# The 1024x1024 weight w3 transposed by DMA instead of TensorE, with the loads ordered behind the transposes

## The chip, the core and the metric

The kernel runs on one core of a Trainium2 chip. A core has TensorE (PE, with PEld for its weight loads), VectorE (DVE), ScalarE (ACT), GpSimd (POOL) and SyncE (SP), and 16 DMA engines that all queues share. Here GpSimd issues the loads from HBM (which cast float32 to bfloat16 on the way), SyncE issues the DMA transposes and almost all stores. The metric is the device time of one execution in microseconds. Before the change it is 581.21 us, the median of 8 runs (580.31 to 581.56).

## The reference

```python
def _attn_ref(q, k, v, tau):            # q, k, v: (4, 5824, 256) float32, tau = 1
    qn = q / (np.linalg.norm(q, axis=1, keepdims=True) + 1e-06)
    kn = k / (np.linalg.norm(k, axis=1, keepdims=True) + 1e-06)
    s = kn.transpose(0, 2, 1) @ qn / tau        # (4, 256, 256)
    s = s - s.max(-1, keepdims=True)
    a = np.exp(s)
    a /= a.sum(-1, keepdims=True) + 1e-09
    return (v @ a)

def _moe_ref(x, w1, w2, w3, w_out):     # x: (23296, 256); w1, w2: (256, 1024)
    a = x @ w1
    b = x @ w2
    h = a * b @ w3                      # (a * b) @ w3, w3: (1024, 1024)
    return (h @ w_out)                  # w_out: (1024, 256)
```

For each of four batches a 256x256 channel attention matrix is formed from q and k (sums over all 5824 rows), applied to v, and a feed-forward layer with a product of two branches follows.

## The kernel before, in words

**Folding.** The kernel never forms x = v @ a. It folds the attention matrix into the two first weights, once per batch: Wf = (softmax matrix) @ [w1, w2], 256 x 2 x 1024 (`fold_mm`, line 337). It also folds the last two weights, once in all: W_sb = w3 @ w_out, 1024 x 256 (`w_unit`, line 567). For that product w3 has to lie transposed in SBUF. So each batch is: a = v Wf1, b = v Wf2, ab = a * b, out = ab W_sb.

**Chunks and steps.** A batch's 5824 rows are 45 tiles of 128 rows and a rest of 64; they are taken in 12 chunks (`NCH`), eleven of 512 columns and a short one of 192. For each chunk there are eight steps j (`emit_ab`, line 413): four TensorE products of 512 columns into two PSUM tiles a and b; ScalarE copies a to SBUF (line 425); VectorE multiplies with b into a bfloat16 tile `ab` (line 428). The out product of a step (`emit_out`, line 438) is four products of 256 columns, issued later: finished `ab` tiles wait in the list `pend`, of which two steps stay (`LAG`). After the eighth step of a chunk ScalarE and VectorE copy the sums out of PSUM and SyncE stores them (512 KB). As long as W_sb is not ready (`w_ready`), `pend` only grows; later up to two out steps per a/b step are issued until it is down to two. 38 `ab` buffers hold this backlog.

**Inputs.** q, k and v come in six pieces per batch (piece = 8 row tiles, 512 KB in bfloat16, the last one shorter): 5 buffers for q, 6 for k, 3 for v. v is needed transposed (vT): a piece is loaded, and SyncE issues a DMA transpose of it (`transpose_piece`, line 149). Pieces 0 and 1 of batch 0 are transposed on TensorE (`transpose_half_on_pe`). vT piece p serves chunks 2p and 2p+1. The buffers of vT are two; the first one holds w3 and w_out in the beginning (`w3_wout`, line 490).

**Order of the work.** The order on each engine is the order of the program; each engine runs its own instructions in order and waits by semaphores. Batch 0's scores are formed at the start, ahead of everything (lines 485 to 556). Then a planner runs: `clock` adds up TensorE's cost in microseconds (a/b step 0.863, out step 0.437), and an agenda (`make_agenda`, line 582) holds side work with a due time on that clock: loads, DMA transposes, the score products of the next batch (`score_units`: 69 units, spread from t0 to t1), its soft-max (`soft_units`), and in batch 0 the transposes of w3 (`w3_transpose`, due from 12 us) and the eight `w_unit` products (due from 24 us). `run_due` issues what is due before each step.

**Gates.** A load would start as soon as GpSimd reaches it. `gate` (line 408) holds it back: GpSimd copies one element of the newest `ab` tile, so GpSimd waits until VectorE has made that tile, and the load that follows in GpSimd's order starts then.

**w3 before.** w3 is loaded in two transfers (line 536), then w_out, then piece 2 of v. `w3_transpose` (line 559) turns each 128-row block by eight TensorE transposes into a PSUM tile of the "ab" buffers, which ScalarE or VectorE (in turn) copies to SBUF: 64 transposes, eight copies. Two halves of the result lie in `sq` buffers, two in a `Wf` buffer.

Of the kernel before, what the change touches and what calls it, by code (L numbers as in the profile page):

```python
# [13 lines left out]
BF16 = DT.bfloat16  # L14

P = 128
# [8 lines left out]
def kernel(  # L25
# [102 lines left out]
    def pe_transpose(dst, src, tag, on_act):  # L128

        m = psum.tile([P, 8, P], BF16, tag=tag, name=f"tr_{nc.get_next_instruction_name()}", bufs={"ab": 4, "out": 3}[tag])  # L130
        for i, blk in enumerate(src):
            nc.tensor.transpose(m[:, i, :], blk, ident_b)
# [256 lines left out]
    def at(t, cost, fn):  # L389
        seq[0] += 1  # L390
        agenda.append((t, seq[0], cost, fn))
# [12 lines left out]
        return vTt[:, ct, :]  # L404

    last_ab = [None]

    def gate():

        if last_ab[0] is not None:  # L410
            nc.gpsimd.tensor_copy(gate_t, last_ab[0][:1, :1])  # L411

    def emit_ab(b, c, j):
        n = chunk_cols(c)
        tiles = []
        for w in range(2):
            t = psum.tile([P, 512], F32, tag="ab", name=f"{'ab'[w]}_{b}_{c}_{j}", bufs=4)
            for ct in range(CT):
                nc.tensor.matmul(  # L419
                    t[:, :n], lhsT=Wf[b][:, ct, w, j * P : (j + 1) * P], rhs=rhs_of(b, c, ct),  # L420
                    start=(ct == 0), stop=(ct == CT - 1),
                )
            tiles.append(t)
        a_sb = work.tile([P, 512], BF16, tag="a_sb", name=f"as_{b}_{c}_{j}", bufs=4)
        nc.scalar.copy(a_sb[:, :n], tiles[0][:, :n])  # L425
        ab = work.tile([P, 512], BF16, tag="ab_sb", name=f"abs_{b}_{c}_{j}", bufs=8 * NDEF + 6)
        if n == 4 * P:
            nc.vector.tensor_mul(ab, a_sb, tiles[1])  # L428
# [50 lines left out]
    def load_qk(n, pi):  # L479
        load_piece("q", n, pi)  # L480
        load_piece("k", n, pi)
# [11 lines left out]
    w3T = {}  # L493

    def new_w3T():

        m = wf_pool.tile([P, 2, 2, FT, P], BF16, tag="Wf", name="w3T_wf")
        for h in range(2):
            w3T[h] = work.tile([P, 2, FT, P], BF16, tag="sq", name=f"w3T_{h}", bufs=2)
            w3T[2 + h] = m[:, h]  # L500

    w3r = moe_w3.rearrange("(jh jl) l -> jl jh l", jl=P)
    w1r = moe_w1.rearrange("(ch cl) f -> cl ch f", cl=P)
# [27 lines left out]
            new_piece("v", 0, 0)  # L531
        load_part("v", 0, 0, h * half, (h + 1) * half)
    load_piece("v", 0, 1)
    for h in range(2):
        js = slice(h * FT // 2, (h + 1) * FT // 2)
        nc.gpsimd.dma_start(out=w3_bf[:, js, :], in_=w3r[:, js, :])
    nc.gpsimd.dma_start(out=wout_sb, in_=moe_w_out.rearrange("(lh ll) c -> ll lh c", ll=P))
    load_piece("v", 0, 2)
    squares("k", 4, whole)
    squares("k", 5, range(LAST + 1), end=True)  # L540
    soft0[0]()
# [12 lines left out]
    busy(4)  # L554
    transpose_half_on_pe(0, 0, 0, False)
    soft0[4]()
    new_w3T()

    def w3_transpose(jt):
        pe_transpose(  # L560
            w3T[jt // 2][:, jt % 2, :, :], [w3_bf[:, jt, lt * P : (lt + 1) * P] for lt in range(FT)],
            "ab", jt % 2 == 0,
        )

    w_ready = [False]

    def w_unit(jt):
# [14 lines left out]
    def make_agenda(b):  # L582
        agenda.clear()
        clock[0] = 0.0
        n = b + 1
        if b == 0:
            for i in range(2):
                at(1.5 + 0.6 * i, 0.43, soft0[5 + i])
            at(4.0, 0.5, lambda: transpose_half_on_pe(0, 0, 1, False))
            at(7.0, 0.5, lambda: transpose_half_on_pe(0, 1, 0, True))  # L590
            at(8.0, 0.5, lambda: transpose_half_on_pe(0, 1, 1, False))
            for jt in range(FT):
                at((12.0 if jt < 4 else 15.0) + jt, 0.5, lambda jt=jt: w3_transpose(jt))
                at(24.0 + jt, 0.87, lambda jt=jt: w_unit(jt))
            at(14.0, 0.0, lambda: transpose_piece(0, 2))
            loads = [("v", 0, 3, 14.0), ("v", 0, 4, 34.0), ("v", 0, 5, 54.0)]
            loads += [("qk", 1, pi, t) for pi, t in enumerate([22.0, 30.0, 40.0, 52.0, 66.0, 80.0])]
            loads += [("v", 1, pi, t) for pi, t in enumerate([96.0, 108.0, 122.0])]
            t0, t1 = 52.0, 120.0
        else:  # L600
            loads = [("v", b, pi, t) for pi, t in [(3, 1.0), (4, 20.0), (5, 34.0)]]
            t0, t1 = 16.0, 104.0
            if n < B:
                loads += [("qk", n, pi, t) for pi, t in enumerate([4.0, 12.0, 27.0, 44.0, 58.0, 72.0])]
                loads += [("v", n, pi, t) for pi, t in enumerate([84.0, 96.0, 108.0])]
        for nm, m, pi, t in loads:
# [68 lines left out]
```

## Time and profile before

| | |
|---|---|
| median of 8 runs | 581.21 us (580.31 to 581.56) |
| the profiled execution, its own time | 581.51 us |
| its span in the profile | 579.1 us |
| TensorE busy | 565.1 us (98%) |
| VectorE, ScalarE, GpSimd busy | 376.8, 341.5, 64.1 us |
| software DMA queue (loads) / hardware queue (stores, transposes) | 39.46 MB / 34.61 MB |
| a, b products, 128x512 | 704 each, 379 ns each by the profile |
| out products, 128x256 | 1440, 273 ns each |
| first a/b step of batch 0, 1, 2 | 40.38, 187.19, 321.39 us |

A matmul's duration in the profile includes its way through the array, and matmuls overlap; what one costs TensorE is read from the distance of starts (two products of 512 columns: 0.43 us). In a timeline line, the first number is the start in us from the span's begin, the second the time, and in brackets stands the idle time before, and what ended it. In a stretch, each engine has its busy time and its number of instructions; then come the granted clock, the DMA engines' share and GB/s. In lists of DMA issues the last number is the median time in us from issue to landing.

### The profile page before, as it was taken

The page shows a single profiled execution, that of the slowest core. Times are in us where ns is not written, and L with a number is a line of the kernel's source. Part 1 is how long each engine was busy: PE and PEld are TensorE (multiplying, and loading weights), DVE is VectorE, ACT ScalarE, POOL GpSimd, SP SyncE. Part 2 cuts the span into 40 slices and gives each one's busy share as a digit, 9 for nine tenths or more (in the row PEclk, how much of TensorE's full clock was granted, in tenths as well). Part 3 has the DMA queues.
Part 4 walks back from the last instruction along what each step waited for, and adds up shares of the span by engine and source line. Part 5 has one row for each costly group of instructions (what it writes and reads, how often), then busy time and mean ns, then how long its engine had stood idle before and what let it go on. Part 6 is the DMA issues. An engine that isn't in the chain of part 4 may idle for free.

```text
span 579.1 us, 10224 instructions
## 1 busy us (share of the span) xinstructions
PE 565.1 (98%) x3826; PEld 360.7 (62%) x3834; DVE 376.8 (65%) x601; ACT 341.5 (59%) x628; POOL 64.1 (11%) x142
## 2 busy tenths in 40 slices
PE   7799999999999999999999999999999999999996
PEld 4665676766656566666666666666665655566664
DVE  0047545888877667788766667778876656565564
ACT  0046535777765566777665566767665555454453
POOL 5240021110000202001000112001100000000000
PEclk9999999999999999999999999999999999999999
DMA  8999989773543899755552699754563335301011
GB/s 163 212 207 199 172 155 204 163 166 77 122 98 109 127 224 176 116 110 125 123 132 74 141 200 173 172 113 87 146 130 89 83 78 144 84 38 74 37 72 55
DMA packets 66113, 74.85 MB, mean 129 GB/s; under 512 B 45840, under 2 KB 49808, under 8 KB 66064
## 3 DMA queue, kind: packets, MB, share of 16 engines
q0 software_dynamic: 15376, 39.46, 40.0%
q1 hardware_dynamic: 50544, 34.61, 20.6%
q8 instruction: 30, 0.49, 0.3%
q14 instruction: 19, 0.16, 0.1%
q10 hardware_dynamic: 144, 0.13, 0.1%
HBM read 78.91 MB, written 23.86 MB: 177 GB/s over the span
## 4 chain that ended last, share of the span: by engine, by line
PE 87%; DMA 7%; ACT 1%; DVE 1%; issue 1%; POOL 1%; ACTq 0%; POOLq 0%
PE o L452 26%; PE a L419 26%; PE b L419 26%; PE G L188 5%; DMA q<-in_q_dram 4%; DMA k<-in_k_dram 2%; PE fold L344 2%; PE w L570 1%; DMA v<-in_v_dram 1%; ACT as L425 1%; DVE abs L428 1%; POOL k L109 0%; DVE osb L473 0%; PE row L272 0%; POOL q L109 0%
## 5 line engine op out<-in xcount | busy, mean ns | idle before, releaser
L428 DVE TENSOR_TENSOR abs<-as,b 128x512 bf16<-128x512 bf16 x352 | 240.4, 685 | 148.6 <-ACT as L425 137.8
L425 ACT CAST as<-a 128x512 bf16<-128x512 f32 (+1 forms) x384 | 215.5, 562 | 173.2 <-PE a L419 84.0
L452 PE MATMUL o<-W_sb,abs 128*128 128x256 bf16 x1440 | 218.1, 273 | 0.5 <-ACT osb L472 0.4
L419 PEld LDWEIGHTS <-Wf 128*128 128x128 bf16 x1536 | 148.9, 98 | 98.1 <-issue 1.7
L419 PE MATMUL a<-vT,Wf 128*128 128x512 bf16 x704 | 209.4, 379 | 0.4
L419 PE MATMUL b<-vT,Wf 128*128 128x512 bf16 x704 | 209.4, 379 | 0.1
L452 PEld LDWEIGHTS <-abs 128*128 128x128 bf16 x1440 | 140.7, 98 | 86.2 <-issue 0.5
L197 DVE TENSOR_TENSOR acc<-acc,sq 128x1024 f32<-128x1024 f32 x66 | 80.4, 1218 | 0.1
L411 POOL COPY gate_t<-abs 1x1 bf16<-1x1 bf16 x39 | 10.3, 265 | 395.6 <-DVE abs L428 387.5
L188 PE MATMUL G<-k,q 128*128 128x256 bf16 x276 | 49.7, 273 | 0.5 <-DMA k<-in_k_dram 0.5
L185 ACT ACTIVATE sq<-q 128x512 f32<-128x512 bf16 x66 | 41.8, 633 | 0.0
L185 ACT ACTIVATE sq<-k 128x512 f32<-128x512 bf16 x66 | 41.6, 631 | 0.0
L473 DVE COPY osb<-o 128x512 f32<-128x512 f32 x44 | 30.1, 684 | 0.4 <-PE o L452 0.4
L188 PEld LDWEIGHTS <-q 128*128 128x128 bf16 x276 | 27.0, 98 | 3.8 <-issue 0.7
L472 ACT COPY osb<-o 128x512 f32<-128x512 f32 x44 | 25.7, 585 | 3.8 <-PE o L452 1.7
L274 ACT ACTIVATE kr<-row 128x256 f32<-128x256 f32 x4 | 1.5, 384 | 31.1 <-PE row L272 31.1
L109 POOL DMA_DIRECT2D q<-in_q_dram x28 | 15.0, 538 | 13.8 <-DMA k<-in_k_dram 5.0
L344 PE MATMUL fold<-w,e 128*128 128x512 bf16 x61 | 16.0, 378 | 0.1
L351 ACT ACTIVATE Wf<-fold,rs 128x512 bf16<-128x512 f32 x16 | 10.9, 687 | 8.4 <-PE fold L344 5.5
L109 POOL DMA_DIRECT2D v<-in_v_dram x25 | 13.4, 539 | 6.7 <-issue 4.9
L109 POOL DMA_DIRECT2D k<-in_k_dram x25 | 13.8, 551 | 3.4 <-DMA k<-in_k_dram 1.9
L353 DVE TENSOR_SCALAR Wf<-fold,rs 128x512 bf16<-128x512 f32 x16 | 11.8, 747 | 2.2 <-PE fold L344 1.8
(103 smaller groups left out, 196.4 us busy)
## 6 DMA issues: line engine op xcount, KB each, us to landing
out_dram<-osb SPq DMA_DIRECT2D x44, 512.0 KB, 3.0
k<-in_k_dram POOLq DMA_DIRECT2D x19, 512.0 KB, 9.2
v<-in_v_dram POOLq DMA_DIRECT2D x19, 512.0 KB, 5.3
q<-in_q_dram POOLq DMA_DIRECT2D x18, 512.0 KB, 6.6
w_wout<-in_moe_w_dram POOLq DMA_DIRECT2D x2, 1024.0 KB, 16.2
k<-in_k_dram POOLq DMA_DIRECT2D x4, 320.0 KB, 6.5
v<-in_v_dram POOLq DMA_DIRECT2D x4, 320.0 KB, 5.2
q<-in_q_dram POOLq DMA_DIRECT2D x4, 256.0 KB, 10.4
```

The source lines that it names most:

```text
L109: nc.gpsimd.dma_start(out=pieces[nm, n, pi][:, lo:hi, :], in_=qk_main[nm, n][0][:, pi * PIECE + lo : pi * PIECE + hi, :])
L185: nc.scalar.activation(out=dst[:, :, part, :], in_=src[:, o : o + 2, :], func=AF.Square)
L188: nc.tensor.matmul(G[:, ct, :], lhsT=qt[:, i, ct * P : (ct + 1) * P], rhs=kt[:, i, :], start=(pr == 0 and part == 0 and ct == 0), stop=(pr ...
L197: nc.vector.tensor_add(accs[n], accs[n], sqs[0])
L344: nc.tensor.matmul(st["fold", i], lhsT=st["e"][:, c2, c1 * P : (c1 + 1) * P], rhs=w12[:, c2, w, h * 512 : (h + 1) * 512], start=(c2 == 0), ...
L353: nc.vector.tensor_scalar_mul(dst, st["fold", i], st["rs"][:, c1 : c1 + 1])
L419: nc.tensor.matmul(t[:, :n], lhsT=Wf[b][:, ct, w, j * P : (j + 1) * P], rhs=rhs_of(b, c, ct), start=(ct == 0), stop=(ct == CT - 1),)
L425: nc.scalar.copy(a_sb[:, :n], tiles[0][:, :n])
L428: nc.vector.tensor_mul(ab, a_sb, tiles[1])
L452: nc.tensor.matmul(tl[s // 2][:, s % 2, :], lhsT=lhsT, rhs=W_sb[:, j, :], start=(j == 0 and s % 2 == 0), stop=(j == FT - 1 and (s % 2 == 1 ...
L472: nc.scalar.copy(o[:, 0:2, :], tl[0])
L473: nc.vector.tensor_copy(o[:, 2:4, :], tl[1])
```

## The change

Six things are done together.

1. w3 is no longer transposed by TensorE. `transpose_w3` issues four DMA transposes on SyncE (each 128 x 2048 elements, the shape of a v piece), at 15 us of the planner's clock, ahead of that of v piece 2. The four results lie in `k` buffers.
2. The loads at the start are reordered: v piece 2, then w_out, then w3 in one transfer instead of two. SyncE's transposes thus wait for all of w3.
3. The `w_unit` products are due from 30 us instead of 24. More `ab` tiles wait in that time, so those of chunks 0 and 1 of batch 0 are put in four of the `q` buffers (four tiles in each).
4. `hold` is new: after a load of v, the next load's gate is preceded by a GpSimd copy of one element of the transposed tile. GpSimd thereby waits until the DMA transpose of that v piece has landed, before it issues the next load. For a load of q and k that follows another one of q and k there is no `hold`.
5. The loads get new due times and a new order (`moves`), and the DMA transpose of a v piece is due 4 us after its load instead of 8.
6. The score units are spread over 58 to 120 us in batch 0 (52 to 120 before) and over 20 to 104 us in the later ones (16 to 104 before).

```diff
@@ emit_ab
+        if b == 0 and c < 2:
+            if j % 4 == 0:
+                held[0] = in_pool.tile([P, 4, 512], BF16, tag="q", name=f"abq_{c}_{j}", bufs=IN_BUFS["q"])
+            ab = held[0][:, j % 4, :]
+        else:
+            ab = work.tile([P, 512], BF16, tag="ab_sb", name=f"abs_{b}_{c}_{j}", bufs=8 * NDEF + 6)
...
+    def hold(src):
+        nc.gpsimd.tensor_copy(gate_t, src)
...
-    def new_w3T():
-        m = wf_pool.tile([P, 2, 2, FT, P], BF16, tag="Wf", name="w3T_wf")
-        for h in range(2):
-            w3T[h] = work.tile([P, 2, FT, P], BF16, tag="sq", name=f"w3T_{h}", bufs=2)
-            w3T[2 + h] = m[:, h]
+    def transpose_w3():
+        for h in range(FT // 2):
+            m = in_pool.tile([P, 2, FT, P], BF16, tag="k", name=f"w3T_{h}", bufs=IN_BUFS["k"])
+            nc.sync.dma_start_transpose(m, w3_bf[:, 2 * h : 2 * h + 2, :])
+            w3T.append(m)
...
     load_piece("v", 0, 1)
-    for h in range(2):
-        js = slice(h * FT // 2, (h + 1) * FT // 2)
-        nc.gpsimd.dma_start(out=w3_bf[:, js, :], in_=w3r[:, js, :])
+    load_piece("v", 0, 2)
     nc.gpsimd.dma_start(out=wout_sb, in_=moe_w_out.rearrange("(lh ll) c -> ll lh c", ll=P))
-    load_piece("v", 0, 2)
+    nc.gpsimd.dma_start(out=w3_bf, in_=w3r)
...
-    def w3_transpose(jt):
-        pe_transpose(
-            w3T[jt // 2][:, jt % 2, :, :], [w3_bf[:, jt, lt * P : (lt + 1) * P] for lt in range(FT)],
-            "ab", jt % 2 == 0,
-        )
...
+            at(15.0, 0.0, transpose_w3)
+            at(15.0, 0.0, lambda: transpose_piece(0, 2))
             for jt in range(FT):
-                at((12.0 if jt < 4 else 15.0) + jt, 0.5, lambda jt=jt: w3_transpose(jt))
-                at(24.0 + jt, 0.87, lambda jt=jt: w_unit(jt))
-            at(14.0, 0.0, lambda: transpose_piece(0, 2))
-            loads = [("v", 0, 3, 14.0), ("v", 0, 4, 34.0), ("v", 0, 5, 54.0)]
-            loads += [("qk", 1, pi, t) for pi, t in enumerate([22.0, 30.0, 40.0, 52.0, 66.0, 80.0])]
-            loads += [("v", 1, pi, t) for pi, t in enumerate([96.0, 108.0, 122.0])]
-            t0, t1 = 52.0, 120.0
+                at(30.0 + jt, 0.87, lambda jt=jt: w_unit(jt))
+            moves = [("v", 0, 3, 29.0), ("qk", 1, 0, 38.0), ("qk", 1, 1, 43.0), ("v", 0, 4, 50.0), ("qk", 1, 2, 58.0)]
+            moves += [("qk", 1, 3, 63.0), ("v", 0, 5, 70.0), ("qk", 1, 4, 81.0), ("qk", 1, 5, 87.0)]
+            moves += [("v", 1, 0, 96.0), ("v", 1, 1, 106.0), ("v", 1, 2, 116.0)]
+            t0, t1 = 58.0, 120.0
         else:
-            loads = [("v", b, pi, t) for pi, t in [(3, 1.0), (4, 20.0), (5, 34.0)]]
-            t0, t1 = 16.0, 104.0
-            if n < B:
-                loads += [("qk", n, pi, t) for pi, t in enumerate([4.0, 12.0, 27.0, 44.0, 58.0, 72.0])]
-                loads += [("v", n, pi, t) for pi, t in enumerate([84.0, 96.0, 108.0])]
+            moves = [("v", b, 3, 1.0), ("qk", n, 0, 10.0), ("qk", n, 1, 16.0), ("v", b, 4, 24.0), ("qk", n, 2, 34.0)]
+            moves += [("qk", n, 3, 40.0), ("v", b, 5, 48.0), ("qk", n, 4, 60.0), ("qk", n, 5, 66.0)]
+            moves += [("v", n, 0, 78.0), ("v", n, 1, 90.0), ("v", n, 2, 100.0)]
+            moves = [m for m in moves if m[1] < B]
+            t0, t1 = 20.0, 104.0
+        before = (0, 2) if b == 0 else None
+        for nm, m, pi, t in moves:
+            if before is not None:
+                at(t, 0.0, lambda w=before: hold(vTs[w[0]][1][:1, 0, :1] if w[1] == NP_ - 1 else vTs[w[0]][0][:1, w[1] * PIECE, 0, :1]))
+            at(t, 0.0, gate)
             if nm == "qk":
-                at(t, 0.0, gate)
                 at(t, 0.0, lambda m=m, pi=pi: load_qk(m, pi))
+                before = None
             else:
-                at(t, 0.0, gate)
                 at(t, 0.0, lambda m=m, pi=pi: load_piece("v", m, pi))
-                at(t + 8.0, 0.0, lambda m=m, pi=pi: transpose_piece(m, pi))
+                at(t + 4.0, 0.0, lambda m=m, pi=pi: transpose_piece(m, pi))
+                before = (m, pi)
```

More of the change, by code (lines that the diff above doesn't have):

```diff
@@ L406 @@
     last_ab = [None]
+    held = [None]
     def gate():
@@ L425, in emit_ab @@
         nc.scalar.copy(a_sb[:, :n], tiles[0][:, :n])
-        ab = work.tile([P, 512], BF16, tag="ab_sb", name=f"abs_{b}_{c}_{j}", bufs=8 * NDEF + 6)
+        if b == 0 and c < 2:
[4 more added lines that the diff above has]
+            ab = work.tile([P, 512], BF16, tag="ab_sb", name=f"abs_{b}_{c}_{j}", bufs=8 * NDEF + 6)
         if n == 4 * P:
@@ L492 @@
     wout_sb = w3_wout[:, FT * F : FT * (F + D)].rearrange("p (l d) -> p l d", d=D)
-    w3T = {}
-    def new_w3T():
-        m = wf_pool.tile([P, 2, 2, FT, P], BF16, tag="Wf", name="w3T_wf")
-        for h in range(2):
-            w3T[h] = work.tile([P, 2, FT, P], BF16, tag="sq", name=f"w3T_{h}", bufs=2)
-            w3T[2 + h] = m[:, h]
+    w3T = []
+    def transpose_w3():
[3 more added lines that the diff above has]
+            w3T.append(m)
     w3r = moe_w3.rearrange("(jh jl) l -> jl jh l", jl=P)
@@ L556 @@
     soft0[4]()
-    new_w3T()
-    def w3_transpose(jt):
-        pe_transpose(
-            w3T[jt // 2][:, jt % 2, :, :], [w3_bf[:, jt, lt * P : (lt + 1) * P] for lt in range(FT)],
-            "ab", jt % 2 == 0,
-        )
     w_ready = [False]
@@ L598, in make_agenda @@
-            loads += [("v", 1, pi, t) for pi, t in enumerate([96.0, 108.0, 122.0])]
-            t0, t1 = 52.0, 120.0
-        else:
-            loads = [("v", b, pi, t) for pi, t in [(3, 1.0), (4, 20.0), (5, 34.0)]]
-            t0, t1 = 16.0, 104.0
-            if n < B:
-                loads += [("qk", n, pi, t) for pi, t in enumerate([4.0, 12.0, 27.0, 44.0, 58.0, 72.0])]
-                loads += [("v", n, pi, t) for pi, t in enumerate([84.0, 96.0, 108.0])]
-        for nm, m, pi, t in loads:
+                at(30.0 + jt, 0.87, lambda jt=jt: w_unit(jt))
```

## The prediction

> **What bounds the kernel now.** I read the page's busy times first, then the stretches, then TensorE's own timeline around the two places that the change touches (the transposes of w3, and the first score product of a batch), then the queues of GpSimd and SyncE, then single landings. Forms, `us` and `ns` are as the views give them.
>
> ```profile
> span 579.1 us, 10224 instructions
> PE 565.1 (98%) x3826; PEld 360.7 (62%) x3834; DVE 376.8 (65%) x601; ACT 341.5 (59%) x628; POOL 64.1 (11%) x142
> ...
> 40.00:76.00 36.00, 35.61 (x262) 21.66 (x261) 23.11 (x37) 21.95 (x37) 3.18 (x8) 1.00 1.03 174
> 76.00:182.00 106.00, 105.57 (x708) 69.03 (x707) 77.38 (x108) 70.83 (x131) 10.93 (x25) 1.00 0.65 143
> 182.00:204.00 22.00, 21.60 (x150) 14.15 (x149) 14.21 (x33) 12.62 (x26) 3.17 (x8) 1.00 0.65 111
> ```
>
> TensorE (first busy column) is full from 40 us to the end at full clock (1.00): over whole stretches it lacks 0.4 us here and there. So an instruction taken off TensorE is worth its time, and any new wait of TensorE costs its whole length. Nothing else is near a bound except in moments.
>
> ```profile
> 52.94 0.61 PE L132 MATMUL tr_I-703_704<-ident_b,w_wout 128*128 128x128 bf16 x8
> 53.38 0.59 PE L419 MATMUL a<-vT,Wf 128*128 128x512 bf16 x2
> ...
> 55.14 0.59 PE L419 MATMUL a<-vT,Wf 128*128 128x512 bf16 x2
> 55.86 0.59 PE L419 MATMUL b<-vT,Wf 128*128 128x512 bf16 x2
> ...
> 187.19 0.59 PE L419 MATMUL a<-vT,Wf 128*128 128x512 bf16 x2
> ...
> 203.00 0.60 PE L452 MATMUL o<-W_sb,abs 128*128 128x256 bf16 x4
> 204.12 0.38 PE L188 MATMUL G<-k,q 128*128 128x256 bf16 x2 [0.52 <-DMA k<-in_k_dram]
> ```
>
> Read starts, not durations: eight transposes hold TensorE for 53.38 - 52.94 = 0.44 us; two products of 512 columns for 0.43, so an a/b step is 0.865. Between 55.14 and 55.86 it is 0.72 instead of 0.43: 0.29 us of waiting for a PSUM buffer. Four output products take 0.436, so the score product should have begun at 203.43; it began at 204.12, 0.69 late, when k had landed. Batch 1 begins at 187.19.
>
> ```profile
> 190.87 0.53 POOL L109 DMA_DIRECT2D v<-in_v_dram  x1 [0.36 <-issue]
> 192.54 0.18 POOL L411 COPY gate_t<-abs 1x1 bf16<-1x1 bf16 x1 [1.15 <-DVE abs L428]
> 193.08 0.53 POOL L109 DMA_DIRECT2D q<-in_q_dram  x1 [0.36 <-ACT as L425]
> 193.60 0.54 POOL L109 DMA_DIRECT2D k<-in_k_dram  x1
> ...
> 58.30 6.84 SPq L155 DMA_TRANSPOSE vT<-v  x2
> ...
> 196.19 7.00 SPq L155 DMA_TRANSPOSE vT<-v  x1
> ```
>
> The DMA view gives landings after issue: the transpose at 196.19, beside q and k, 12.3 us; one alone, at 157.44, 3.6. A v piece 5.3 (190.87). k 10.5 at 193.60; 7.5 undisturbed (218.06); 9.4 beside a store of the output (248.87), 8.5 in another such place (382.61).
>
> **The change part by part.** Durations are of the profiled execution: span 579.1, its own time 581.51, so 2.4 lie around the span; it stands 0.3 above the median of 581.21, against which I state the result.
>
> *Transposes of w3 leave TensorE.* 8 x 8 transposes go: 8 x 0.435 = 3.5 us, all on the path. With them go four ScalarE copies of 1.01 us and four VectorE copies of 0.68, which held PSUM buffers: the timeline from 53 to 66 us shows four gaps, 0.29 + 0.17 + 0.29 + 0.29 = 1.04 us, each at a step that follows such a copy. Bounds 3.5 and 4.5; I take 4.5, because the a/b steps without transposes, from 40.4 to 52.9, show no gap.
>
> *Four DMA transposes on SyncE instead, ahead of that of v piece 2.* The loads are reordered (v piece 2, w_out, then w3 in one transfer), the bytes are the same, and the last load landed at 58.3 (SyncE's first transpose waited for it). So w3 lands near 58.3. Two transposes back to back (issued 58.30 and 62.46, landed 7.1 and 4.8 later, so 65.4 and 67.3) show a pitch of 1.9. Here no load runs beside, since the next one waits: 58.3 + 3.6 = 61.9 for the first, + 4 x 1.9 to 2.0 = 69.5 to 69.9 for the fifth, v piece 2. It is needed at the first step of chunk 4: 40.38 + 32 steps x 0.865 + 2 folds x 0.432 + 3 transposes of v x 0.435 = 70.2. The products with w3 come one step later and need transposes that landed from 61.9 to 67.9. (SyncE's queue holds nothing else by then; the transposes of v, now issued 4 instead of 8 us after their loads on the planner's clock, wait for the loads in any case.) So the cover is 0.3 us wide. Bounds: 0, and the 3.5 by which a load beside it delayed the transpose at 58.30 (7.1 against 3.6); I take 0.2, being nearest to the pair's pitch. Behind on SyncE stand the transpose of v piece 3 and the stores, not due before 90 us.
>
> *The output product begins later*: the eight products of w3 and w_out move from 24 to 30 us of the planner's clock, so 35 instead of 23 steps queue up. The same instructions run; TensorE has a/b steps in place of them. Sixteen tiles of the first two chunks lie in four q buffers; the first is wanted again by q piece 1 at 43 us, when the first four outputs have been emitted, the last by piece 3 at 63. Nothing on the path.
>
> *Batch 0's score units* go into 58 to 120 instead of 52 to 120 us: 69 units, 62 us. VectorE then has per us 23/62 sums of 1.22 us and 0.64 steps of 0.77: 0.95, before 0.92. The last five folds fall into the short chunk 11. Bounds 0 and the 1.0 us of gaps that the same soft-max stretch and chunk 11 show now; I take 0.3.
>
> *Every load issue waits for the last DMA transpose* (a GpSimd copy of 0.18 us from the transposed tile, ahead of the gate). Queued behind it on GpSimd: gate, q, k; score product and squares wait for these. In batch 0 the loads come 20 us ahead of need, hidden. In batches 1 and 2 they do not:
> - batch 1: v piece 3 is issued 190.87 - 187.19 = 3.7 us in, as before; + 5.3 landed; + 3.6 transposed, 12.6; + 1.0 for two copies and the issue (0.18 + 0.3 + 0.18 + 0.36), q at 13.6, k 0.5 later. A store of chunk 0 runs beside: k lands 9.0 to 9.9 after q's issue, 22.6 to 23.5. The score product, moved from 16 to 20 on the planner's clock, falls due at 9.75 (chunk 0) + 8 x 1.30 = 20.15 (that clock held to 0.01 us: 203.43 - 187.19 = 16.24 for 16.25). Late by 2.9, less the 0.69 paid now: +2.2.
> - batch 2 begins at 321.39; v at 324.04, 2.65 in; q at 12.55; k at 21.6 to 22.5; due at 20.36: +1.65 (nothing paid now).
> Sum 3.85. Low bound: k undisturbed, 8.0 after q: 0.76 + 0.2 = 0.95. High bound: v 6.2 (324.04), transpose 4.0 (144.99), k 10.5 + 0.5: 1.9 more each, 7.6. I take 3.85, since the store is there.
>
> The trace shows q, k and a transpose slowing each other (12.3 against 3.6 us). [...]
>
> Sum: -4.5 + 0.2 + 0.3 + 3.85 = -0.15 us, 581.1.
>
> **The rivals.**
> - *The k wait is longer, slower*: at the high bound, -4.5 + 0.5 + 7.6 = +3.6, 584.8. It decides (over 0.2%) from 1.3 us over my value in the two batches together, that is k landing about 0.65 later each. For: k at 10.0 to 10.9 in five places; against: these had a transpose beside, which the wait excludes.
> - *Piece 2 of v late, slower*: 3.5 us at chunk 4 in place of 0.2, +3.15, 584.4. For: a cover of 0.3 us; against: SyncE alone with the DMA engines.
> - *k undisturbed, faster*: -4.5 + 0.5 + 0.95 = -3.05, 578.2. For: 7.5 where no store is near; against: the store of chunk 0 is ready about 13.5 us in.
> - *Loads and transposes hidden, w3's transposes were hidden too*: excluded, TensorE has no idle time there.
>
> **How the numbers follow.** Forecast (gain and waits cancel, within 0.2% or 1.2 us, about what a measurement of this kernel tells from no change) 0.38; k wait longer 0.27; v piece late 0.10; k undisturbed 0.25. Faster 0.25, same 0.38, slower 0.37. Range 578.4 to 584.8: from just inside the undisturbed case to the high bound of the k wait; the forecast's own is 580.0 to 582.4.
>
> **What the profile of the changed kernel would show.** No transposes of w_wout on TensorE and no gap before 70 us; five SyncE transposes from about 58 to 68 us; chunk 4 beginning near 70.2; in batches 1 and 2 the first score product waiting 3 and 1.7 us for k; nothing like that in batch 0. Wrong if w3 lands after 60, if the fifth transpose lands after 71, if k lands 8 us or over 11 us after q's issue, or if VectorE, at 0.95, holds TensorE up between 145 and 160 us.

## The result, and the profile after

The changed kernel takes 586.32 us (median of 11 runs, 583.08 to 587.89), the kernel before 580.64 (31 runs, 580.05 to 581.56, on the same chips). The ratio is 1.0084, 95% interval 1.0071 to 1.0096: slower. The forecast was 581.1 with a range of 578.4 to 584.8; the time lies above the range. The profiled execution of after took 586.32 us, its span is 584.5 us, 5.4 longer than before.

From the page of after, the span, the busy times and the granted clock (40 slices, tenths of full speed):

```profile
span 584.5 us, 10135 instructions
...
PE 564.7 (97%) x3762; PEld 358.0 (61%) x3770; DVE 375.4 (64%) x597; ACT 338.4 (58%) x624; POOL 72.8 (12%) x159
...
PEclk9999999999999999999999979999999999999999
```

TensorE has 64 instructions fewer and yet almost the same busy time (564.7 against 565.1 us), and one slice stands at 7 in the clock's row. That is the first sign of something that no term of the forecast holds. The stretches of after (the columns as before: each engine's busy time, then the granted clock, the DMA share, GB/s):

```profile
40.00:76.00 36.00, 34.77 (x190) 17.25 (x189) 26.58 (x40) 22.78 (x39) 0.91 (x3) 1.00 0.99 181
...
330.00:360.00 30.00, 26.86 (x154) 15.74 (x152) 15.09 (x22) 15.30 (x27) 3.34 (x9) 0.89 0.66 144
```

TensorE lacks 1.2 us in the first stretch, and 3.1 us in the last one, where the clock is 0.89 on average. TensorE's waits, as the view of waits counts them (total, times, longest):

```profile
PE G L188 <- DMA k<-in_k_dram: 5.6, 2, 3.1
...
PE a L424 <- DMA vT<-v: 1.2, 1, 1.2
```

And TensorE's timeline of after at the three places:

```profile
70.13 0.59 PE L424 MATMUL b<-vT,Wf 128*128 128x512 bf16 x2
71.95 0.60 PE L424 MATMUL a<-vT,Wf 128*128 128x512 bf16 x2 [1.23 <-DMA vT<-v]
...
204.58 0.60 PE L463 MATMUL o<-W_sb,abs 128*128 128x256 bf16 x4
207.63 0.38 PE L188 MATMUL G<-k,q 128*128 128x256 bf16 x2 [2.45 <-DMA k<-in_k_dram]
...
340.93 0.60 PE L463 MATMUL o<-W_sb,abs 128*128 128x256 bf16 x4
344.66 0.58 PE L188 MATMUL G<-k,q 128*128 128x256 bf16 x2 [3.14 <-DMA k<-in_k_dram]
345.04 1.06 PE L424 MATMUL a<-vT,Wf 128*128 128x512 bf16 x2
345.90 1.06 PE L424 MATMUL b<-vT,Wf 128*128 128x512 bf16 x2
```

Read the starts again. Two products of 512 columns hold TensorE for 0.43 us; from 70.13 to 71.95 it is 1.82, so chunk 4 begins 1.39 late. Four output products hold it 0.44: the score product of batch 1 is 2.62 late (207.63 - 204.58 - 0.44, rounded), that of batch 2 3.30. After the second one the starts stand 0.86 apart instead of 0.43: TensorE runs at half clock, from 343.5 to 350.4 by the clock's record (granted clock 0.51 in that stretch). The surplus of all distances in that stretch is 2.72 us. After the first k wait (207.63) nothing of the kind happens.

The account, each term from the distance of TensorE's starts less their usual one:

| us | before | after | difference |
|---|---|---|---|
| 64 transposes of w3, and the gaps behind their copies | 3.5 + 1.04 | 0.13 | -4.4 |
| chunk 4 waits for v piece 2 | 0 | 1.39 | +1.4 |
| gaps in chunk 11 of batch 0 | 0.26 | 0.69 | +0.4 |
| wait for k, batch 1 | 0.69 | 2.62 | +1.9 |
| wait for k, batch 2 | 0 | 3.30 | +3.3 |
| half clock after it | 0 | 2.72 | +2.7 |
| sum | | | +5.3 |

It leaves 0.1 of the 5.4 us open. The queues of after, GpSimd's (POOL) and SyncE's (SPq):

```profile
58.59 8.20 SPq L510 DMA_TRANSPOSE w3T<-w_wout  x4
66.84 12.62 SPq L155 DMA_TRANSPOSE vT<-v  x2
...
188.47 0.53 POOL L109 DMA_DIRECT2D v<-in_v_dram  x1 [0.33 <-issue]
197.54 0.18 POOL L416 COPY gate_t<-vT 1x1 bf16<-1x1 bf16 x1 [8.55 <-DMA vT<-v]
...
198.29 0.53 POOL L109 DMA_DIRECT2D q<-in_q_dram  x1 [0.34 <-issue]
...
323.62 0.53 POOL L109 DMA_DIRECT2D v<-in_v_dram  x1 [0.34 <-issue]
334.61 0.18 POOL L416 COPY gate_t<-vT 1x1 bf16<-1x1 bf16 x1 [10.46 <-DMA vT<-v]
```

Batch 1 goes as the forecast had it: v issued at 188.47, `hold` (L416) released at 197.54, q at 198.29, k landed 8.8 after its issue. In batch 2 the hold is released 11.0 after v's issue instead of 9.1.

The runs of after differ more than those of before, and their granted clock goes with it (twelve executions, one more than the median has): at 0.997 to 1.000 five lie between 583.1 and 584.1 us and one at 585.1; at 0.992 five between 586.3 and 587.1; at 0.987 one at 587.9. So even with no half clock in the later batches the kernel is some 2.5 to 4.5 us slower than before.

### The profile page after: what moved, and what is told of

The parts are those of the page before. It is cut to its first block, busy times and chain, and to the rows that moved or that the text cites. A ratio compares the mean times of both kernels' runs of the same rounds, so it can differ in the third digit from the quotient of the medians.

```text
span 584.5 us, 10135 instructions
## 1 busy us (share of the span) xinstructions
PE 564.7 (97%) x3762; PEld 358.0 (61%) x3770; DVE 375.4 (64%) x597; ACT 338.4 (58%) x624; POOL 72.8 (12%) x159
## 4 chain that ended last, share of the span: by engine, by line
PE 82%; DMA 13%; issue 1%; ACT 1%; DVE 1%; POOL 1%; SPq 0%; ACTq 0%; POOLq 0%
PE o L463 25%; PE a L424 24%; PE b L424 24%; PE G L188 5%; DMA q<-in_q_dram 4%; DMA v<-in_v_dram 3%; DMA k<-in_k_dram 3%; DMA vT<-v 2%; PE fold L344 2%; PE w L571 1%; ACT as L430 1%; DVE abs L439 0%; POOL q L109 0%; POOL k L109 0%; DVE osb L484 0%
## 5 line engine op out<-in xcount | busy, mean ns | idle before, releaser
L439 DVE TENSOR_TENSOR abs<-as,b 128x512 bf16<-128x512 bf16 x336 | 229.6, 685 | 148.2 <-ACT as L430 128.2
L463 PE MATMUL o<-W_sb,abs 128*128 128x256 bf16 x1376 | 210.8, 273 | 0.5 <-ACT osb L483 0.4
L463 PEld LDWEIGHTS <-abs 128*128 128x128 bf16 x1376 | 134.9, 98 | 82.0 <-issue 1.7
L412 POOL COPY gate_t<-abs 1x1 bf16<-1x1 bf16 x39 | 12.9, 332 | 218.2 <-DVE abs L439 217.4
L416 POOL COPY gate_t<-vT 1x1 bf16<-1x1 bf16 x15 | 4.6, 307 | 162.1 <-DMA vT<-v 162.1
```

Source lines behind the costliest of these rows:

```text
L463: nc.tensor.matmul(tl[s // 2][:, s % 2, :], lhsT=lhsT, rhs=W_sb[:, j, :], start=(j == 0 and s % 2 == 0), stop=(j == FT - 1 and (s % 2 == 1 ...
```

## The experiments

Unless told otherwise, each is the changed kernel with the edit shown, and ratios are to the kernel before (580 to 581 us), with 95% intervals.

### 1. Do the k waits and what follows them make the kernel slower?

The score units of batches 1 and 2 are made due later, and nothing else.

```diff
-            t0, t1 = 20.0, 104.0
+            t0, t1 = 26.0, 104.0
```

> The changed kernel, with the score units of the later batches spread over 26 to 104 us instead of 20 to 104. Theory A (the loss is the wait for k at the first score product of batches 1 and 2, 2.62 and 3.30 us, and the 2.72 us that TensorE then loses at half clock): k lands 22.7 and 23.6 us into its batch, the unit falls due near 26, both waits and the half clock go, 584.5 - 8.6 = about 576 us of span, ratio to before about 0.994, and no run with a granted clock below 0.997. Theory B (the loss is in the longer queue of ab tiles or in denser score units, which become denser still here): no faster than the changed kernel without a clock drop, ratio 1.004 or more.

Measured: 577.53 us (577.41 to 578.13), ratio 0.9946 [0.9928, 0.9964]. The span is 575.8. The stretches of this kernel around the first score products of batches 1 and 2:

```profile
182.00:215.00 33.00, 32.79 (x208) 19.83 (x206) 19.55 (x36) 18.10 (x35) 4.05 (x11) 1.00 0.72 152
320.00:350.00 30.00, 30.00 (x189) 18.36 (x188) 17.28 (x27) 17.00 (x30) 4.05 (x11) 1.00 0.78 166
```

TensorE is full and at full clock, no wait for k is left, and the other terms stay (1.34 us at chunk 4). So the whole loss of the changed kernel, and 3 us more, lies in the waits of batches 1 and 2 and what follows them: 586.3 becomes 577.5, a change of 8.8 us, for 2.62 + 3.30 + 2.72 = 8.6 in the account.

### 2. How much of the k waits is due to `hold`?

```diff
-            if before is not None:
-                at(t, 0.0, lambda w=before: hold(...))
```

> The changed kernel without any of the holds: a load waits only for its gate, so q and k of batches 1 and 2 run beside the transpose of v piece 3 again. Theory A1 (transpose and loads slow each other as much as the hold delays): q is issued about 12.2 us into the batch instead of 13.4 to 14.4, k lands at about 23, waits within 1 us of the changed kernel's. [...]

Measured: 583.36 us (581.87 to 585.46, 10 runs), ratio 1.0044 [1.0031, 1.0058]. GpSimd's queue and TensorE in the timeline of this kernel:

```profile
188.74 0.53 POOL L109 DMA_DIRECT2D v<-in_v_dram  x1 [0.36 <-issue]
...
197.47 0.53 POOL L109 DMA_DIRECT2D q<-in_q_dram  x1 [0.36 <-PE o L463]
...
207.16 0.38 PE L188 MATMUL G<-k,q 128*128 128x256 bf16 x2 [1.73 <-DMA k<-in_k_dram]
```

q goes out 8.73 us after v instead of 9.82. The score products wait 1.89 us (for 2.62) and 2.12 us (for 3.30), with no half clock after them. The hold thus costs 0.7 and 1.2 us of waiting in the profiled execution, 1.9 together, and in batch 2 the wait of 3.30 us with the hold is followed by half clock, that of 2.12 us without it is not. That execution is the shortest of the ten (581.87); by the medians, 586.32 and 583.36, the holds cost 3.0 us. Had the transpose and the loads slowed each other as much as the hold delays (theory A1), it would cost nothing; k took 9.1 and 9.4 us from its issue without the holds and 8.8 and 8.7 with them.

Nor do the holds protect the transposes of w3 in batch 0: without them SyncE is at these four for 8.02 us (8.20 in after), and chunk 4 begins 1.45 late (1.39 in after). v piece 3 then goes out at 71.55 us by its due time alone, when these four have landed (the last at 70.5).

For transposes beside loads these runs go both ways: less waiting without the hold here, and 59 us instead of 8 for a row beside loads in experiment 5.

### 3. Is the half clock an effect of idle TensorE?

Fourteen matmuls of zeros into a PSUM tile that nobody reads are issued ahead of the first score product of batches 1 and 2. They fill the waits without shortening them. (The computation is complete; this is added work.)

```diff
+        if b > 0:
+            at(t0, 0.0, lambda: busy(14))
```

> The changed kernel, with 14 products of zeros (3.0 us) on TensorE ahead of the first score unit of batches 1 and 2; nothing else. They stand where TensorE waited 2.62 and 3.30 us for k, so the end should come no earlier by the wait. Theory C (TensorE's idleness of about 3 us is what takes the clock to half afterwards): the wait turns into work of the same length, the clock stays full in every execution: span 584.5 - 2.7 + 0.4 = 582.2, all executions between 583 and 585. Rival (the half clock comes by chance or from the load): some executions at 586 and above with a granted clock of 0.992, as in the changed kernel.

Measured: 583.76 us (583.48 to 584.98), ratio 1.0057 [1.0044, 1.0070], clock 0.998 to 1.000 in all five runs. The timeline of TensorE, then, in a second fence, the stretch that held the half clock in after:

```profile
205.07 3.18 PE L209 MATMUL warm_I-2611_2612<-warm 128*128 128x512 bf16 x14
208.09 0.38 PE L188 MATMUL G<-k,q 128*128 128x256 bf16 x2
```

```profile
344.00:351.00 7.00, 7.00 (x46) 4.38 (x45) 2.79 (x5) 4.50 (x8) 0.70 (x2) 1.00 0.78 186
```

Useless products make the kernel 2.6 us faster than the changed one. The score product comes no earlier (208.09, for 207.63), but the clock stays at 1.00. So the half clock in after's batch 2 comes from TensorE's idleness (it is gone where the wait is filled, in all five runs), and it costs the 2.7 us of the account. The 583.8 us that are left are what most runs of after took whose clock was not lowered (five of six between 583.1 and 584.1).

**Which waits were followed by half clock?** Those of which the length was read, after 40 us, from the distance of starts less the usual one (the last two by the idle time of the line):

| wait of TensorE, us | where | clock behind it |
|---|---|---|
| 1.30 to 1.45 | chunk 4, after and experiments 1, 2 and 8 | full |
| 1.68 | batch 2, experiment 8 | full |
| 1.89, 2.12 | batches 1 and 2, experiment 2 | full |
| 2.62 | batch 1, after | full |
| 2.64 | batch 1, experiment 5 (order) | half, 1.55 us lost |
| 2.75 | batch 2, experiment 4 | full |
| 2.77 | batch 1, experiment 9 | half |
| 2.88 | batch 1, experiment 4 | half, 1.4 us lost |
| 3.12 | batch 2, experiment 5 (order) | half, 1.66 us lost |
| 3.30 | batch 2, after | half, 2.72 us lost |
| 3.40 | batch 2, experiment 9 | half |
| 3.73 | batch 0, experiment 6 (only q and k held) | full |
| 10.4 | batch 0, experiment 6 (all loads held) | half, for 3.5 us |
| 15.7 | batch 0, experiment 5 (part alone) | half: eight products of 256 columns took 1.89 us, 1.04 ahead of it |

Between 2.62 and 3.73 us it went both ways, so the length alone does not decide. What else does is not shown by these runs.

### 4. The k waits with w3 left on TensorE

```diff
-            at(15.0, 0.0, transpose_w3)
+            at(15.0, 0.0, new_w3T)
...
+                at(20.0 + jt, 0.5, lambda jt=jt: w3_transpose(jt))
```

> The changed kernel, but w3 is transposed on TensorE again (64 transposes, eight PSUM copies, due from 20 us on the planner's clock, results in the same k buffers); loads, waits and units stay. If the DMA transposes are worth what the row says: 8 x 0.435 = 3.5 us more, 0 to 1 us of gaps at the copies, less the 1.39 us wait for v piece 2 at chunk 4, which no longer stands behind four transposes: +2 to +3 us against the changed kernel in the same clock state. If the transposes of w3 on TensorE were hidden: -1.4 us.

Measured: 585.54 us (585.31 to 587.12), ratio 1.0087 [1.0067, 1.0106]. The wait at chunk 4 is gone, since v piece 2 is then alone on SyncE. The waits for k are 2.88 and 2.75, as they must be if they have nothing to do with w3, and the first one is followed by half clock (1.4 us lost). The profiled execution is the longest of the four (587.12), its span 585.1 us. Less the two waits and the half clock that is 578 us; the span of after, 584.5, less its waits (1.39, 2.62, 3.30) and its half clock (2.72) is 574.5. So the DMA transposes are worth about 3.5 us of TensorE, less the 1.39 us at chunk 4.

### 5. The wait at chunk 4, and what the DMA transposes need

**The order of five transposes.** v piece 2 is needed at the same time as w3's first block, and stood fifth.

```diff
-            at(15.0, 0.0, transpose_w3)
             at(15.0, 0.0, lambda: transpose_piece(0, 2))
+            at(15.0, 0.0, transpose_w3)
```

> The changed kernel, with the DMA transpose of v piece 2 issued ahead of the four of w3 (order of two agenda entries swapped). Theory A: piece 2 lands about 52 us and is transposed before w3 is there, the 1.39 us wait at chunk 4 goes; w3's last transpose lands near 71.5 and its product comes at about 78, so nothing else waits: -1.4 us, all else equal. Rival (the wait at chunk 4 only moves to the products with w3): 0.

Measured: 584.58 us (583.75 to 586.01), ratio 1.0067 [1.0045, 1.0089]. No wait at chunk 4, and no other in its place: the products of w3 and w_out start in time. This run also shows the clock at its sharpest; TensorE's timeline at batch 1:

```profile
203.12 0.60 PE L463 MATMUL o<-W_sb,abs 128*128 128x256 bf16 x4
206.19 0.59 PE L188 MATMUL G<-k,q 128*128 128x256 bf16 x2 [2.47 <-DMA k<-in_k_dram]
206.57 1.06 PE L424 MATMUL a<-vT,Wf 128*128 128x512 bf16 x2
...
209.50 0.60 PE L424 MATMUL a<-vT,Wf 128*128 128x512 bf16 x2
```

A wait of 2.64 us, 0.02 longer than that of after, is followed here by half clock: from 206.57 to 209.13 the starts stand 0.85 to 0.86 apart, from 209.50 on 0.43. Both waits of this kernel are (2.64 and 3.12 us; 1.55 and 1.66 us lost).

**w3's transposes alone.** The kernel before, with w3 loaded last and transposed by DMA (v piece 2 first) and its products due at 30; all other loads, gates and score units as before, no hold.

```diff
-                at((12.0 if jt < 4 else 15.0) + jt, 0.5, lambda jt=jt: w3_transpose(jt))
-                at(24.0 + jt, 0.87, lambda jt=jt: w_unit(jt))
+                at(30.0 + jt, 0.87, lambda jt=jt: w_unit(jt))
             at(14.0, 0.0, lambda: transpose_piece(0, 2))
+            at(14.0, 0.0, transpose_w3)
```

> The kernel before with one part of the change alone: w3 (loaded last, in one transfer) goes through four DMA transposes behind that of v piece 2, results in k buffers, its products with w_out due from 30 us; loads, gates and units stay as before. Theory A: the transposes of w3 are worth 3.5 us and up to 1.0 us of gaps, and the loss of the change sits in its other parts: span 579.1 - 4.5 + (0 to 1.5 for products with w3 that wait, because v piece 3, q and k load beside the transposes) = 575 to 576.5, ratio 0.992 to 0.995. Rival (the transposes need the loads held back): they stretch beside the loads (12.3 against 3.6 us in the kernel before), the products wait 3 us or more and the clock drops: ratio 0.998 or more.

Measured: 609.42 us (599.89 to 620.62, 6 runs); the ratio of the three shorter ones is 1.0374 [1.0329, 1.0420]. The expected gain of the part alone did not come; the kernel is 19 to 40 us slower. The timeline of SyncE, GpSimd and TensorE in the profiled execution, the longest of the six, and then the stretches:

```profile
59.69 58.96 SPq L499 DMA_TRANSPOSE w3T<-w_wout  x4
...
61.61 0.56 POOL L109 DMA_DIRECT2D v<-in_v_dram  x1 [5.59 <-DMA vT<-v]
...
64.21 0.54 POOL L109 DMA_DIRECT2D q<-in_q_dram  x1 [0.35 <-PE a L419]
...
89.62 1.89 PE L560 MATMUL w<-w_wout,w3T 128*128 128x256 bf16 x8 [15.73 <-DMA w3T<-w_wout]
```

```profile
76.00:93.00 17.00, 3.38 (x15) 2.03 (x16) 0.00 (x0) 0.96 (x2) 0.00 (x0) 0.60 1.24 99
93.00:123.00 30.00, 4.60 (x25) 2.94 (x23) 1.37 (x3) 0.37 (x1) 0.70 (x2) 0.55 1.21 90
```

SyncE is at the same four transposes for 59 us that take 8.2 us in after. TensorE waits 41.1 us for them, most of it at a lowered clock (0.60 and 0.55 in the two stretches), while the DMA engines are full (share above 1.2) and move only 90 to 99 GB/s, less than the 181 GB/s of after's stretch from 40 to 76 us. Loads of v, q and k go out beside them from 61.6 us on. In after no load goes out between 58.6 and 72.7 us.

### 6. Is it the loads beside the transposes?

The last kernel again, with one hold: GpSimd waits for the last transpose of w3 before it loads v piece 3, and so before all that is queued behind that load.

```diff
+    def hold():
+        nc.gpsimd.tensor_copy(gate_t, w3T[-1][:1, 0, 0, :1])
...
             else:
+                if (m, pi) == (0, 3):
+                    at(t, 0.0, hold)
                 at(t, 0.0, gate)
```

> The kernel before with only w3's DMA transposes (that of v piece 2 ahead of them), as in the run where this part stood alone, and one thing more: GpSimd's load of v piece 3, and with it every load of q and k behind it, waits until the last transpose of w3 has landed. Theory A (the four transposes took 59 us there because loads ran beside them): the row takes 8 to 9 us again, the products of w3 and w_out wait for nothing, the clock stays at full, and what is left is the gain of TensorE: span 579.1 - 4.5 = 574.6 and up to 1 us more from the crowding of the loads that now start together near 70 us; 576.5 to 578 us. Rival (the order of the transposes, or the buffers, made the row slow): the row stays above 30 us and the time above 595.

Measured: four executions of 576.3, 576.8, 589.8 and 591.3 us; the ratio of the two shorter ones is 0.9927 [0.9907, 0.9947]. The timeline of the profiled one (589.8):

```profile
59.85 7.95 SPq L503 DMA_TRANSPOSE w3T<-w_wout  x4
77.21 23.60 SPq L155 DMA_TRANSPOSE vT<-v  x2
100.91 2.19 SPq L478 DMA_DIRECT2D out_dram<-osb  x2
...
71.32 0.18 POOL L415 COPY gate_t<-w3T 1x1 bf16<-1x1 bf16 x1 [34.65 <-DMA w3T<-w_wout]
...
122.25 0.59 ACT L476 COPY osb<-o 128x512 f32<-128x512 f32 x1 [11.42 <-DMA out_dram<-osb]
...
122.89 1.44 PE L456 MATMUL o<-W_sb,abs 128*128 128x256 bf16 x6 [10.39 <-ACT osb L476]
```

The row takes 7.95 us again, and TensorE waits for nothing of w3: one hold takes away the 41 us. So the loads beside the row are the cause, not its order or its buffers, and the gain of this part is there in the two shorter executions (576.3 and 576.8, where 576.5 to 578 was expected). What I had not expected is the next victim. All held loads now start together near 72 us, the transposes of v beside them hold SyncE from 77.2 to 100.8, the stores of the output stand behind these in SyncE's queue and then take 22.5 us to land, and ScalarE waits 11.4 us for the buffer that is being stored; TensorE waits 10.4 us; behind the wait it runs at half clock for 3.5 us (the two products at 124.54 take 0.86 from start to start instead of 0.43), and the granted clock of the execution is 0.991. Of the two longer executions only one has a trace; that the other has the same cause is assumed.

**Only q and k held**, so that v piece 3 alone is loaded beside the row:

```diff
             if nm == "qk":
+                if (m, pi) == (1, 0):
+                    at(t, 0.0, hold)
                 at(t, 0.0, gate)
```

> The same, but only the first load of q and k waits for the last transpose of w3; that of v piece 3 runs beside the row. Theory A1 (any load beside a row stretches it by about its own time): 5 us more, the last transpose at 74 to 76, before the products of w3 and w_out are due (near 75), so no or a small wait of TensorE: 576.5 to 580. Theory A2 (one load beside is enough to break the row, as 12.3 us for one transpose beside q and k hints): the row takes 20 us or more, TensorE waits 8 us or more for w3, and the time is above 585.

Measured: 583.45 us (580.47 to 584.61, 4 runs), ratio 1.0053 [1.0036, 1.0069]. The timeline of the profiled execution (580.47):

```profile
59.90 18.94 SPq L503 DMA_TRANSPOSE w3T<-w_wout  x4
...
77.43 1.05 PE L564 MATMUL w<-w_wout,w3T 128*128 128x256 bf16 x8 [3.57 <-DMA w3T<-w_wout]
```

Neither expectation holds. The last transpose landed at 81.0 instead of 71.3, so a load that takes 5.1 us alone delays the row by about 10 us: more than its own length, and far less than what the six loads of 512 KB did that went out beside the row in experiment 5, without holds. TensorE waits 3.73 us here (3.57 by the idle time of the line). Behind this wait the clock stays full (starts 0.43 apart from 78.32 on, 0.999 over the execution); the other three runs, at a clock of 0.992 to 0.994, are 2.6 to 4.1 us longer (they have no trace).

### 7. Batch 0 of the change, without its later batches

After with v piece 2 transposed first, and due times, order and gates of the loads and units of batches 1 to 3 as before the change, no holds there.

```diff
-            moves = [("v", b, 3, 1.0), ("qk", n, 0, 10.0), ("qk", n, 1, 16.0), ("v", b, 4, 24.0), ("qk", n, 2, 34.0)]
...
-            t0, t1 = 20.0, 104.0
+            moves = [("v", b, 3, 1.0), ("v", b, 4, 20.0), ("v", b, 5, 34.0)]
+            moves += [("qk", n, pi, t) for pi, t in enumerate([4.0, 12.0, 27.0, 44.0, 58.0, 72.0])]
+            moves += [("v", n, 0, 84.0), ("v", n, 1, 96.0), ("v", n, 2, 108.0)]
+            moves = [m for m in moves if m[1] < B]
+            t0, t1 = 16.0, 104.0
```

> The changed kernel's batch 0 (with the transpose of v piece 2 ahead of w3's), and the later batches as before the change: due times of loads and score units as before, no waiting of loads for transposes there. Theory A (the change gains in batch 0 and loses only by the k waits of batches 1 and 2 and the clock after them): 579.1 - 4.5 + 0.4 (the denser score units of batch 0) = 575.0 of span, 577.0 to 578 us, with the 0.69 us wait of batch 1 as before and no half clock. Rival (the denser loads of batch 0 or the later output product cost later too): above 579.

Measured: 576.29 us (576.06 to 576.59), ratio 0.9923 [0.9908, 0.9938], span 574.5. The stretches:

```profile
40.00:76.00 36.00, 36.00 (x200) 18.27 (x198) 26.57 (x40) 23.65 (x41) 0.90 (x3) 1.00 1.09 187
...
330.00:360.00 30.00, 30.00 (x196) 18.93 (x194) 21.75 (x30) 20.82 (x39) 5.24 (x11) 1.00 0.99 194
```

TensorE is full, the later batches wait for nothing. The half of the change that concerns batch 0 is worth 4.6 us (579.1 to 574.5). That is, to 0.1, the -4.4 and +0.4 of the account and the 0.69 us that before waits for k in batch 1 and this kernel does not; the expectation, 575.0, had kept that wait. The half that concerns the later batches, which serves no purpose for w3, loses 8 to 9.

### 8. Two more versions that beat both kernels

q and k of the next batch ahead of v piece 3 in batches 1 and 2, the rest as after:

```diff
-            moves = [("v", b, 3, 1.0), ("qk", n, 0, 10.0), ("qk", n, 1, 16.0), ...
+            moves = [("qk", n, 0, 1.0), ("v", b, 3, 10.0), ("qk", n, 1, 16.0), ...
```

> The changed kernel, with the first q and k pieces of the next batch loaded at 1 us of the later batches and v piece 3 at 10 us (their order swapped); units still from 20 us, holds kept. Theory A (k is late because it stands behind the load and the transpose of v piece 3): k lands about 12 us into the batch, both waits and the half clock go, span 576, as in e1. Theory B (score units at 20 us are the cost, or k would be late anyway): waits of 2 us or more stay.

Measured: 577.76 us (577.51 to 578.98), ratio 0.9952 [0.9939, 0.9965]. The waits at the first score products are gone. In the profiled execution (578.98) one of 1.68 us stands at 369.62 in batch 2: now it is k piece 2, loaded behind v piece 4 and its hold, that comes late (it landed at 369.57). The wait of chunk 4 stays (1.30 us).

Score units of the later batches from 26 us, v piece 2 transposed first, batch 0's units from 54 to 117 us:

```diff
-            at(15.0, 0.0, transpose_w3)
             at(15.0, 0.0, lambda: transpose_piece(0, 2))
+            at(15.0, 0.0, transpose_w3)
...
-            t0, t1 = 58.0, 120.0
+            t0, t1 = 54.0, 117.0
...
-            t0, t1 = 20.0, 104.0
+            t0, t1 = 26.0, 104.0
```

> The changed kernel with all found losses taken out: score units from 26 us in the later batches (as in e1), v piece 2 transposed ahead of w3 (as in e3), and batch 0's score units 3 to 4 us earlier (54 to 117 us), so that its folds come before the short chunk 11, where they now cost 0.43 us. Theory A: 575.8 (e1) - 1.34 - 0.4 = about 574 of span, 576 us, ratio 0.992, better than both kernels. Rival (VectorE is the bound once the rest is gone): 575.5 or more of span.

Measured: 575.58 us (575.36 to 576.02), ratio 0.9911 [0.9898, 0.9924], span 573.7, clock 1.0. It is the fastest of the study, 5 us below before and nearly 11 below the changed kernel, with all of its DMA transposes and holds.

### 9. Why was the wait of batch 2 longer than that of batch 1?

In twelve profiles the load of v at the begin of batch 2 took 6.2 to 7.2 us, at that of batches 1 and 3 5.0 to 5.3. Only at the begin of batch 2 do two stores of 64 KB run beside it (the rests of two batches). They are moved away, to 45 us of batch 2's clock.

```diff
+                    rest = work.tile([P, D], F32, tag="rest", name=f"rest_{b}", bufs=1)
+                    nc.vector.tensor_copy(rest, tl[0][:, 1, :])
...
+        if b == 2:
+            at(45.0, 0.0, lambda: rests.pop()())
```

> The changed kernel with one thing moved: the two stores of 64 KB (the rests of 64 rows of batches 0 and 1), which ran beside the load of v piece 3 at the begin of batch 2, are issued at 45 us of batch 2's clock instead; for the tile that holds them one of the 38 ab buffers is given up. Theory (these stores are what made that load take 6.2 to 7.2 us in every profile, against 5.0 to 5.3 where they are absent): v lands 5.0 to 5.3 us after its issue, the score product of batch 2 waits 1.2 to 1.9 us instead of 3.3, no half clock follows it; 586.3 - 1.7 - 2.7 = 581.9, or 583 to 584 where the wait of batch 1 (2.6 us) brings the half clock by itself. Rival (the load is slow there for another reason, the place in the batch or the store of the last chunk): v still takes 6.2 us or more, the wait stays at 2.5 us or more, 584 to 587.

Measured: 585.16 us (582.60 to 589.97, 10 runs), ratio 1.0086 [1.0059, 1.0112]. The list of DMA issues (number, size, us to landing) at the begin of batch 2, of after and, in the second fence, of this kernel:

```profile
v<-in_v_dram POOLq DMA_DIRECT2D x1, 512.0 KB, 7.2
out_dram<-osb SPq DMA_DIRECT2D x1, 128.0 KB, 2.1
out_dram<-osb SPq DMA_DIRECT2D x2, 64.0 KB, 6.2
```

```profile
v<-in_v_dram POOLq DMA_DIRECT2D x1, 512.0 KB, 6.3
out_dram<-osb SPq DMA_DIRECT2D x1, 128.0 KB, 2.0
```

The rival's signs came, all three: v took more than 6.2 us, the wait is no shorter, 3.40 us, and the time lies between 584 and 587. v landed 0.9 us sooner than in after, not 1.9, and as the profiles with the two stores already differ by 1.0, one profile does not show that these stores matter at all. The 128 KB store of the short chunk, issued 0.1 us after v, is still beside it; in batch 1 it goes out 1.1 us ahead. The wait is as long as before because of k: the 512 KB store of chunk 0 now goes out 0.4 us after q (337.43 and 337.04; in after 0.5 ahead of it) and takes 8.5 us instead of 2.7, and k lands 9.7 after its issue instead of 8.7. Why v is slow there stays open; whether it is the 128 KB store was not tried.

## Why the prediction was wrong, point by point

- **Transposes of w3 leave TensorE, -4.5.** Right: -4.4 by the account. Where batch 0's part stands alone, the sum of this, the +0.4 of chunk 11 and the missing k wait of 0.69 is -4.7, for -4.6 measured (experiment 7).
- **Four DMA transposes ahead of v piece 2, +0.2.** Mis-sized: 1.39. The fifth landed at 71.9, not at 69.5 to 69.9. The mechanism was right (the cover of 0.3 us was too thin), the bounds of 0 and 3.5 held it. The five landed at 62.5, 64.5, 67.1, 70.4 and 71.9, a pitch of 2.35 us on average where the sum had 1.9 to 2.0, taken from a pair. Times four, that is 1.6 us; the first one came 0.6 later than the sum had it. A landing after 71 was one of the prediction's own signs of being wrong.
- **Batch 0's denser units, +0.3.** Right: +0.43, in chunk 11 where it was expected.
- **k wait of batch 1, 2.9 late.** Right: 2.62. Each step of the chain (v 5.3, transpose 3.6, 1.0 for the copies, k 8.8 beside the store) came within 0.2 us.
- **k wait of batch 2, 1.65.** Mis-sized by half: 3.30. The sum took v's landing of batch 1 (5.3) for both batches, though the trace of before had 6.2 at exactly this place; the value appeared only in the high bound. It was 7.2, which none of the rows cited had. The rows of the same place, not the more frequent one, were the right ones to take.
- **Loads and a transpose slow each other.** Rightly read, a transpose of 12.3 us beside q and k against 3.6 alone, but it does not make the hold free in the later batches, where it cost 0.7 and 1.2 us (experiment 2). The score product waits for k alone: in batch 1 k was issued 9.25 us after v without the hold and took 9.1, with it 10.34 us after v, and took 8.8.
- **The step that failed is the price of a wait**: "any new wait of TensorE costs its whole length". The sum has no term beyond the length. TensorE's clock was taken as given at 1.00 because the stretches that were read showed that; before had no wait above 0.69 us there, so its trace could not show it. What the runs showed in its place is 2.72 us at half clock behind the wait of 3.30, half of the 5.2 us by which the forecast missed. Without it the miss would have been 2.5 us, inside the range; this rest is mainly the two mis-sized terms above, 1.65 in batch 2 and 1.2 at chunk 4.
- **The rival "k wait is longer"** named the mechanism and the side, with 3.6 us at its high bound. The waits for k came to 5.23 more than before, inside its 7.6; together with chunk 4 and the clock, which it did not hold, the time passed it. Its high bound was also added up wrongly. The values it names (v 6.2, transpose 4.0, k 10.5 + 0.5) are 0.9 + 0.4 + 1.55 = 2.85 us above the values taken, not 1.9, so it would be about 9.5 instead of 7.6 and the range would end near 586.8. The time would then lie inside, but by luck: that sum has no term for the clock either.
- **The rival "k undisturbed"** and its 578.2 show what the change would be worth with its loads in time: 577.5 was measured with the units moved (experiment 1).

## What to carry to other kernels

Price a new wait of a full TensorE at its length, and then look at the granted clock behind it: behind waits of 2.64 to 3.30 us half clock took another 1.4 to 2.7 us where it followed, and it did not follow each of them. A wait of 3.30 us cost 6.0 here, and a few useless products in the wait, or work due 6 us later, were cheaper. When work moves to DMA transposes, ask first what loads run beside the row, and keep these loads away only there, by a hold or by their due time. With the loads due as before the change one hold was worth 41 us of waiting in batch 0; with the due times of the change none was needed there; and holds at the two places where a load is on the path cost 1.9 us of waiting, 3.0 us by the medians. Take each landing from the row of the same place in the program, with the same stores beside it.

## What the runs showed of the hardware

- Behind TensorE's waits of 2.64, 2.77, 2.88, 3.12, 3.30 and 3.40 us after 40 us the granted clock was half (in after from 343.5 to 350.4 us); behind those of 1.30 to 2.12, of 2.62, 2.75 and 3.73 us it was full. With the waits filled by products of zeros it was 0.998 to 1.000 in all five runs (experiment 3).
- A row of four DMA transposes of 512 KB took SyncE 8 us with nothing beside, 19 us with one load of 512 KB beside, and 59 us with six such loads of v, q and k beside (one profile each of the last two); the DMA engines then counted as full at 90 to 99 GB/s. Loads suffered too: in the last case q and k had median landings of 40 and 42 us, instead of 7 to 10.
- A store of 512 KB that landed in 2.7 us when issued 0.5 us ahead of a q load took 8.5 when issued 0.4 us behind it (one case each).
